# New pitches, latencies and planner settings for the static instruction order of a two-layer linear-attention and gated-MLP kernel

**The chip, the cores and the metric.** The kernel runs on one core of one Trainium2 chip. The metric is the device time of one execution in microseconds. The profiled span, from the first to the last instruction of the core, is about 1.7 us shorter (1109.5 us in the run that took 1111.19 us).

## The reference

Two identical layers act on 2048 tokens of width 576: a linear attention with 32 heads of 18, then a gated MLP of inner width 4608. Shortened:

```python
phi_q = concat(softmax(pq), softmax(-pq))      # pq = q @ w_phi per head, head width 18
phi_k = concat(softmax(pk), softmax(-pk))
kv  = einsum("bhsf,bhsd->bhfd", phi_k, v);  z = phi_k summed over s
o   = (phi_q @ kv) / (phi_q @ z + 1e-6)
...
x = x + attention(layernorm(x), wqkv, w_phi, wo)
h = (layernorm(x) @ w_gate) * (layernorm(x) @ w_up)
x = x + h @ w_down
# the four lines are applied twice, with the same weights
```

The MLP needs all of kv, and so all 16 token tiles of 128, before its first block can start. Hence a "K phase" stands ahead of the first MLP, and a long stream of matmuls after it. Layer 2's attention is interleaved with the MLP of layer 1.

## The kernel before

The kernel is not written as loops over engines. Each task (a K tile, a query tile, an MLP block) is a generator that yields instructions with what they read and write. At build time a list scheduler walks through all of them with a model of the time, always takes the instruction whose estimated start (less a bias by priority) is the earliest, and appends it to the order of its engine. The chip then runs these fixed orders, with semaphores between the engines. The model's numbers therefore never cost anything on the chip; they only choose an order.

```python
SEM_LAT = 64.0                 # result of any engine is seen by any other after 64 ns
def ready_time(self, deps, eng=None):
    for d in deps:
        f = self.fin.get(d, 0.0) + (PE_SELF if eng == "pe" and d[0] == "pe" else SEM_LAT)
        ...
# an "alt" request: the planner may pick the engine
e_ = max(self.free_at[eng], tr.ready_time(deps), th.t_ready)
f_ = e_ + sum(o.dur for o in ops) * self.alt_cost[eng]     # earliest end wins; the first listed wins a tie
```

The softmax of one K tile, where the changed subtraction sits (the numbers are planned durations in ns):

```python
def softmax_front(self, st_, pz, Wm, km, crit, ...):
    # projection on TensorE into two PSUM banks, two ScalarE copies to SBUF (psb), then:
    VectorE  max of the SBUF copy (line 1030), 2 x min from PSUM (line 1035)
    GpSimd   d1 = psb - max            (line 1040, 1150)
    ...
    if crit == 1 and s.sub2pool:       # False before
        yield ("alt", [("dve", ops), ("pool", [Op(1150, d2 = psb - min)])])   # line 1054
    else:
        yield ("ops", "dve", ops)      # ops = 2 x 370: d2 = PSUM - min, line 1049
def softmax_tail(self, sm, crit, pz=None):
    ScalarE  exp of d2, exp of d1      (lines 1109, 1111)
    VectorE  sums of both              (line 1117)
    if crit > 1: VectorE reciprocal (line 1121)   else: ScalarE ln, exp (line 1124)
    GpSimd (or, if crit > 1, GpSimd or VectorE) 2 scalings   (line 1128)
    # afterwards TensorE accumulates K-V products of the tile (line 1170)
```

In one MLP block TensorE fills PSUM banks with gate and up products (line 1428, row-split: two 64-row matmuls run side by side), ScalarE copies the gate (line 1474), and VectorE multiplies it with the up product (line 1476), which frees the banks. Query projections (line 990 on the whole array, line 1002 row-split) are either done in the K phase or left to fill the MLP stream.

## Time and profile before

| what | before |
|---|---|
| time, median of 3 runs | 1112.03 us (1111.32 to 1113.44) |
| first gate/up matmul (line 1428) | 116.65 us |
| from there to the last epilogue (line 1544) | 989.1 us |
| layer-1 gate/up blocks 2 to 5, counted from 0, first to last matmul | 41.89 us (block 3: 42.09) |
| query tiles projected before the first gate/up matmul | 11 |

The prediction below shows the page, the stage table, and the waits of before. The chain of waits, the sequence of work that ended last, restricted to the K phase, can be followed back from 117 us to 56.5 us. Columns: start in us, length in us, engine, tile, line and number of instructions.

```profile
61.41 3.53 PE ps L990 x15
64.96 0.40 ACT psbx L1027
65.88 2.30 POOL dd L1128 x2
68.22 0.77 PE ps L1170 x10
...
81.75 1.26 DVE ss L1117
83.02 0.66 DVE mxmnx L1030
83.67 0.73 DVE mxmnx L1035 x2
...
99.93 1.75 POOL dd L1128
101.72 0.77 PE ps L1170 x10
102.49 1.23 PE ps L990 x10
```

The reader is to see three stretches. From 61 to 81 us TensorE, GpSimd, ScalarE and VectorE take turns. From 81 to 100 us every piece is VectorE. From 100 to 116.65 us it is one GpSimd scaling, then nearly only TensorE. Added up over the pieces from 56.5 to 116.65 us, VectorE has about 24 us of this chain, TensorE 25, GpSimd 6 and ScalarE 4. So VectorE is busy for 92% of the K phase, but it carries about 40% of the visible part of what sets its end. (The first piece is long for another reason: from 61.1 to 64.5 us the trace records a granted TensorE clock of 0.5. Ten such matmuls take 1.23 us elsewhere in this chain, so fifteen would take about 1.85 us instead of 3.53. The section on the experiments comes back to this.)

### The profile page before, as it was taken

The numbers are of one execution on the slowest core, as the hardware profiler recorded it, in microseconds if no ns is written. First come the engines' busy times: TensorE is split into PE (matmuls) and PEld (weight loads), VectorE is DVE, ScalarE is ACT, GpSimd is POOL, SyncE is SP. The second block draws the span as 40 slices with busy tenths as digits, with TensorE's granted clock in tenths as the row PEclk, the third lists the DMA queues.
The fourth block names the chain that finished last, engine by engine and source line by source line (L and its number), as shares of the span: only waits on it lengthen the run. The fifth ranks groups of instructions, "written<-read, shape, count | busy, mean of one in ns | idle before, by whom it ended". The sixth has DMA issues, their size and how long they took to land.

```text
span 1109.5 us, 33782 instructions
## 1 busy us (share of the span) xinstructions
PE 1072.4 (97%) x15342; PEld 832.2 (75%) x15342; DVE 586.1 (53%) x1192; ACT 373.7 (34%) x855; POOL 311.4 (28%) x330
## 2 busy tenths in 40 slices
PE   6787999999999999999999899999999999999998
PEld 4565886868687786869687678696969696969685
DVE  8998744646375564636453675444435353524231
ACT  6776631414133242404232463131313130402120
POOL 4885512414152432413220252211212130300000
PEclk9999999999999999999999999999999999999999
DMA  7595227273552616371523313727172726262504
GB/s 169 121 279 194 38 44 195 48 205 47 149 100 78 162 29 194 48 204 27 159 69 96 98 24 47 215 36 216 36 215 35 205 47 188 63 182 48 180 26 140
DMA packets 185002, 129.07 MB, mean 116 GB/s; under 512 B 103322, under 2 KB 183706, under 8 KB 183706
## 3 DMA queue, kind: packets, MB, share of 16 engines
q1 hardware_dynamic: 184858, 126.91, 44.6%
q8 instruction: 120, 1.97, 0.7%
q14 instruction: 24, 0.20, 0.1%
HBM read 100.75 MB, written 2.36 MB: 93 GB/s over the span
## 4 chain that ended last, share of the span: by engine, by line
PE 87%; DVE 4%; DMA 1%; ACT 1%; POOL 1%; issue 0%
PE ps L1428 50%; PE ps L1501 22%; PE ps L1002 7%; PE ps L1503 3%; PE ps L990 2%; PE ps L1289 2%; PE ps L1170 1%; DVE ss L1117 1%; POOL dd L1128 1%; DVE x_sb L1364 1%; DMA oT<-dd 1%; DMA wdr<-in_B_w_down_dram 0%; DMA wdx<-in_B_w_down_dram 0%; DVE mxmn L1035 0%; DVE dd L1049 0%
## 5 line engine op out<-in xcount | busy, mean ns | idle before, releaser
L1428 PE MATMUL ps<-xT,Wu 64*128 64x256 bf16 x4608 | 581.8, 269 | 0.0
L1428 PE MATMUL ps<-xT,Wg 64*128 64x256 bf16 x4608 | 579.2, 269 | 0.8 <-ACT xT L972 0.8
L1428 PEld LDWEIGHTS ps<-xT,Wu 64*128 64x128 bf16 x4608 | 431.5, 94 | 22.0 <-DVE hT L1476 0.3
L1428 PEld LDWEIGHTS ps<-xT,Wg 64*128 64x128 bf16 x4608 | 427.4, 94 | 27.4 <-issue 3.3
L1474 ACT CAST hT<-ps 128x512 bf16<-128x512 f32 x288 | 168.4, 585 | 568.5 <-PE ps L1428 541.7
L1476 DVE TENSOR_TENSOR hT<-ps,hT 128x512 bf16<-128x512 f32 x288 | 198.3, 690 | 240.7 <-ACT hT L1474 238.9
L1501 PE MATMUL ps<-wdr,hT 128*128 128x512 bf16 x960 | 245.2, 380 | 1.0 <-DMA wdr<-in_B_w_down_dram 1.0
L1503 PE MATMUL ps<-wdr,hT 128*128 128x64 bf16 x960 | 185.0, 193 | 0.0
L1428 PE MATMUL ps<-xT,Wr 64*128 64x256 bf16 x1152 | 184.9, 269 | 0.0
L1501 PEld LDWEIGHTS ps<-wdr,hT 128*128 128x128 bf16 x960 | 93.9, 98 | 111.1 <-DMA wdr<-in_B_w_down_dram 1.8
L1128 POOL TENSOR_TENSOR dd<-dd,ss 128x576 bf16<-128x576 bf16 x119 | 137.1, 1174 | 123.0 <-ACT ss L1124 119.0
L1099 POOL TENSOR_TENSOR dd<-xT,mxq 128x576 bf16<-128x576 bf16 x56 | 63.5, 1163 | 329.4 <-DVE mxq L1095 329.4
L1544 DVE TENSOR_TENSOR x_sb<-ps,x_sb 128x64 bf16<-128x64 f32 x32 | 7.0, 220 | 228.6 <-PE ps L1503 228.6
L962 POOL TENSOR_SCALAR xln<-x_sb,nmean,rstd 128x576 bf16<-128x576 bf16 x100 | 61.1, 616 | 182.1 <-ACT rstd L951 103.7
L1503 PEld LDWEIGHTS ps<-wdr,hT 128*128 128x128 bf16 x960 | 94.1, 98 | 0.2
L1117 DVE TENSOR_REDUCE ss<-dd 128x64 f32<-128x1152 bf16 x61 | 81.9, 1344 | 15.1 <-ACT dd L1111 15.0
L1428 PEld LDWEIGHTS ps<-xT,Wr 64*128 64x128 bf16 x1152 | 78.1, 94 | 5.2
L1501 PE MATMUL ps<-wdx,hT 128*128 128x512 bf16 x192 | 54.3, 380 | 0.1
L1109 ACT ACTIVATE dd<-dd 128x576 bf16<-128x576 bf16 x61 | 41.7, 684 | 32.8 <-DVE dd L1049 22.7
L1040 POOL TENSOR_TENSOR dd<-psb,mxmn 128x576 bf16<-128x576 bf16 x26 | 30.3, 1166 | 64.8 <-DVE mxmn L1030 64.8
L934 DVE BATCH_NORM_STATS2 st<-x_sb 128x6 f32<-128x288 bf16 x120 | 45.9, 444 | 2.4 <-DMA x_sb<-in_A_x_dram 2.4
L1002 PE MATMUL ps<-Wo,oT 64*128 64x288 bf16 x504 | 44.0, 283 | 1.2 <-DMA oT<-dd 0.4
(123 smaller groups left out, 970.0 us busy)
## 6 DMA issues: line engine op xcount, KB each, us to landing
wdr<-in_B_w_down_dram SPq DMA_DIRECT2D x240, 288.0 KB, 3.7
wdx<-in_B_w_down_dram SPq DMA_DIRECT2D x48, 288.0 KB, 3.7
Wg<-in_B_w_gate_dram SPq DMA_DIRECT2D x4, 1152.0 KB, 17.0
Wu<-in_B_w_up_dram SPq DMA_DIRECT2D x4, 1152.0 KB, 19.5
x_sb<-in_A_x_dram SPq DMA_DIRECT2D x8, 288.0 KB, 3.4
out_dram<-x_sb SPq DMA_DIRECT2D x16, 144.0 KB, 2.7
Wraw<-in_A_wqkv_dram SPq DMA_DIRECT2D x8, 144.0 KB, 2.8
xT<-xln SPq DMA_TRANSPOSE x58, 2.6
```

Source lines behind the costliest of these rows:

```text
L934: ops.append(Op(d_dve(288), (lambda e, j=j, h=h, src=src: e.bn_stats(st[:, sl[j], 6 * h:6 * h + 6], src)), reads=rd, writes=[("st", sl[j], ...
L962: em = [(lambda e, j=j, a=a, b=b, c=c: e.tensor_scalar(xln[:, sl[j], a:b], x_sb[:, ss[j], c:c + b - a], s.nmean[:, sl[j]:sl[j] + 1], rstd[ ...
L1002: out.append(Op(61, (lambda e, h=h, k=k, st=(i == 0 and k == 0), sp=(i == 1 and k == 3): e.matmul(s.ps[:, banks[h], 0:N], L[r, k, :], Wm[r ...
L1099: yield ("ops", "pool", [Op(1150, (lambda e, d=d, mb=mb: e.tensor_tensor(d, p3, mb, ALU.subtract)), reads=[("xT", st_), ("mq", mq, br)], w ...
L1109: yield ("ops", "act", [Op(590, (lambda e: e.activation(de2, de2, ACTF.Exp, scale=-1.0)), reads=s.ddk(sm, 1), writes=s.ddk(sm, 1))])
L1117: Op(1320, (lambda e: e.tensor_reduce(ss[:, sm, :].rearrange("p (b g) -> p b g", b=2), e4, AX.X, ALU.add)), reads=s.ddk(sm, 0) + s.ddk(sm, ...
L1128: yield ("alt", [(eng, [Op(dur, (lambda e, ev=ev, rb=rb: e.tensor_tensor(ev, ev, rb, ALU.mult)), reads=s.ddk(sm, br) + [("ss", sm)], write ...
L1428: out.append(Op(54.3, (lambda e, bank=bank, cs=cs, lhsT=lhsT, rhs=rhs, st=st, sp=sp: e.matmul(ps[:, bank, cs].rearrange("p (a n) -> p a n" ...
L1474: yield ("ops", "act", [Op(540, (lambda e, gb=gb, p=p: e.copy(hT[:, p, :], ps[:, gb, :])), reads=[("gu", gb)], writes=[("hT", p)] + (s.raw ...
L1476: yield ("ops", "dve", [Op(625, (lambda e, ub=ub, p=p: e.tensor_tensor(hT[:, p, :], ps[:, ub, :], hT[:, p, :], ALU.mult)), reads=[("gu", u ...
L1501: ops = [Op(d_pe(512), (lambda e: e.matmul(s.ps[:, bank, 0:512], lhsT, s.wslot(slot)[:, fi, 0:512], start=(f == 0), stop=(f == NF - 1))), ...
L1503: Op(d_pe(64) + 3, (lambda e: e.matmul(s.ps[:, z, 64 * sl:64 * sl + 64], lhsT, s.wslot(slot)[:, fi, 512:576], start=(f == 0 and (sl == 0 o ...
```

## The change

Its intent: the planner should know, for every engine, how long an instruction occupies it (pitch) apart from how long its result takes to be seen (latency); and the second subtraction of a K tile may go to GpSimd. The planner's settings were chosen anew with it. Core of the diff (cuts marked):

```diff
-SEM_LAT = 64.0
+LAT = {"pe": 200.0, "act": 145.0, "dve": 120.0, "pool": 90.0, "sp": 64.0}
-            f = ... (PE_SELF if eng == "pe" and d[0] == "pe" else SEM_LAT)
+            f = ... (PE_SELF if eng == "pe" and d[0] == "pe" else LAT.get(d[0], 64.0))
 def d_act(n, psum=False, ptrs=0):
-    return n / 1.2 + (63.0 if psum else 92.0) + 93.0 * ptrs
+    return n / 1.2 + 50.0
 def d_actc(n):
-    return n / 1.2 + 155.0
+    return n / 1.2 + 50.0
@@ settings
-        self.qlead = 8;  self.alt = 1.2; self.lnlead = 14; self.pqp = (5, 5); self.pqg = 12
+        self.qlead = 7;  self.alt = 1.1; self.lnlead = 9;  self.pqp = (3, 3); self.pqg = 6
-        self.qcrit = False; self.fq = 3; self.fqs = 2; self.fqp = 7.5; self.sub2pool = False
+        self.qcrit = True;  self.fq = 5; self.fqs = 1; self.fqp = 6.5; self.sub2pool = True
@@ planned durations: query max/min 720 -> 665, both exponentials 590 -> 560, sums 1320 -> 1265,
@@ gate copy 540 -> 480, gate product 625 -> 600   (each is one number in the code)
```

"Model" below means the latencies and durations, "settings" the two lines under it.

More of the change, by code (lines that the diff above doesn't have):

```diff
@@ L67, in ready_time @@
         for d in deps:
-            f = self.fin.get(d, 0.0) + (PE_SELF if eng == "pe" and d[0] == "pe" else SEM_LAT)
+            f = self.fin.get(d, 0.0) + (PE_SELF if eng == "pe" and d[0] == "pe" else LAT.get(d[0], 64.0))
             if f > t:
@@ L556, in __init__ @@
         self.early = (2, 2)
-        self.qlead = 8
-        self.alt = 1.2
-        self.wage = 0.0
+        self.qlead = 7
+        self.alt = 1.1
+        self.wage = 0
         self.lnage = 4
-        self.lnlead = 14
+        self.lnlead = 9
         self.pol0 = 1
@@ L564, in __init__ @@
         self.urgent = 4
-        self.pqp = (5, 5)
-        self.pqg = 12
+        self.pqp = (3, 3)
+        self.pqg = 6
         self.NPQ = 2
@@ L570, in __init__ @@
         self.pqn = (16, 16)
-        self.qcrit = False
-        self.fq = 3
-        self.fqs = 2
-        self.fqp = 7.5
-        self.sub2pool = False
+        self.qcrit = True
+        self.fq = 5
+        self.fqs = 1
+        self.fqp = 6.5
+        self.sub2pool = True
         self.rboost = 500.0
@@ L1094, in stored_front @@
         for br, alu in ((0, ALU.max), (1, ALU.min)):
-            yield ("ops", "dve", [Op(720, (lambda e, br=br, alu=alu: e.tensor_reduce(s.mxq[:, mq, br, :], p3, AX.X, alu)), reads=[("xT", st_)], writes=[("mq", mq, br)])])
+            yield ("ops", "dve", [Op(665, (lambda e, br=br, alu=alu: e.tensor_reduce(s.mxq[:, mq, br, :], p3, AX.X, alu)), reads=[("xT", st_)], writes=[("mq", mq, br)])])
         for br in range(2):
@@ L1108, in softmax_tail @@
         de2 = dd[:, sm, 1, :]
-        yield ("ops", "act", [Op(590, (lambda e: e.activation(de2, de2, ACTF.Exp, scale=-1.0)),
+        yield ("ops", "act", [Op(560, (lambda e: e.activation(de2, de2, ACTF.Exp, scale=-1.0)),
                                  reads=s.ddk(sm, 1), writes=s.ddk(sm, 1))])
-        yield ("ops", "act", [Op(590, (lambda e: e.activation(de1, de1, ACTF.Exp)),
+        yield ("ops", "act", [Op(560, (lambda e: e.activation(de1, de1, ACTF.Exp)),
                                  reads=[("dd", sm, 0)], writes=[("dd", sm, 0)])])
@@ L1116, in softmax_tail @@
         yield ("ops", "dve", [
-            Op(1320, (lambda e: e.tensor_reduce(ss[:, sm, :].rearrange("p (b g) -> p b g", b=2), e4, AX.X, ALU.add)),
+            Op(1265, (lambda e: e.tensor_reduce(ss[:, sm, :].rearrange("p (b g) -> p b g", b=2), e4, AX.X, ALU.add)),
                reads=s.ddk(sm, 0) + s.ddk(sm, 1), writes=[("ss", sm)]),
@@ L1473, in t_bmain @@
                     p = 2 * q + i
-                    yield ("ops", "act", [Op(540, (lambda e, gb=gb, p=p: e.copy(hT[:, p, :], ps[:, gb, :])),
+                    yield ("ops", "act", [Op(480, (lambda e, gb=gb, p=p: e.copy(hT[:, p, :], ps[:, gb, :])),
                                              reads=[("gu", gb)], writes=[("hT", p)] + (s.raw_keys if (L, b) == (1, 0) else []), excl=[("pb", gb)])])
-                    yield ("ops", "dve", [Op(625, (lambda e, ub=ub, p=p: e.tensor_tensor(hT[:, p, :], ps[:, ub, :], hT[:, p, :], ALU.mult)),
+                    yield ("ops", "dve", [Op(600, (lambda e, ub=ub, p=p: e.tensor_tensor(hT[:, p, :], ps[:, ub, :], hT[:, p, :], ALU.mult)),
                                              reads=[("gu", ub), ("hT", p)], writes=[("hT", p)], excl=[("pb", ub)])])
```

## The prediction

> **What bounds the kernel now.** I read, in order: the page's engine totals, the 40 slices, a table of engine time by stage, the groups of instructions before and after 117 us, the timelines of VectorE and GpSimd between 60 and 105 us, and the waits of TensorE after 117 us.
>
> ```profile
> PE 1072.4 (97%) x15342; PEld 832.2 (75%) x15342; DVE 586.1 (53%) x1192; ACT 373.7 (34%) x855; POOL 311.4 (28%) x330
> ...
> PE   6787999999999999999999899999999999999998
> DVE  8998744646375564636453675444435353524231
> POOL 4885512414152432413220252211212130300000
> ```
>
> TensorE is busy 97% of the span; only the first four slices (28 us each) and the middle dip are lower. VectorE is at 80 to 90% only in those four slices. So there are two regimes, which the stage table separates:
>
> ```profile
> 5.00:30.00 25.00, 18.69 (x120) 12.73 (x120) 22.40 (x66) 18.11 (x53) 10.89 (x14) 1.00 0.74 174
> 30.00:60.00 30.00, 23.46 (x207) 16.84 (x207) 28.43 (x58) 21.61 (x59) 26.70 (x26) 0.94 0.51 112
> 60.00:102.00 42.00, 33.44 (x297) 24.18 (x298) 38.45 (x65) 30.76 (x82) 30.46 (x27) 0.96 0.80 266
> 102.00:117.00 15.00, 14.36 (x148) 10.67 (x147) 11.01 (x27) 9.56 (x24) 4.95 (x5) 1.00 0.35 110
> ```
>
> Columns: stretch, length, then busy time of PE, PEld, DVE, ACT and POOL, clock, DMA. From 5 to 102 us (the "K phase": norm, K and V projection, both softmax branches and the K-V product of 16 tiles) VectorE is busy 89.3 of 97 us. Its longest waits in that stretch are 1.5 us or less and together 9 us. From 102 to 117 us runs a dependent chain (last K-V product, block-diagonal state, numerators of tiles 0 and 1, output projection, norm, transpose); the first gate/up matmul starts at 116.65 us. After that TensorE waits only a little:
>
> ```profile
> PE ps L990 <- ACT xT L972: 1.6, 2, 0.8
> PE ps L1501 <- DMA wdr<-in_B_w_down_dram: 1.0, 2, 0.8
> PE ps L1428 <- ACT xT L972: 0.8, 1, 0.8
> PE ps L1344 <- ACT oT L1326: 0.6, 1, 0.6
> PE ps L990 <- ACT oT L1326: 0.5, 1, 0.5
> ```
>
> These five and three smaller ones are 5.7 us of waiting in 990 us. Everything after 117 us is a stream of matmuls, so only fewer matmuls in it, or an earlier start of it, shorten the program.
>
> The matmuls that could leave that stream are query projections of layer 1. Before 117 us:
>
> ```profile
> L990 PE MATMUL ps<-Wq,xT 128*128 128x288 bf16 x110 | 15.7, 287 | 2.8 <-DVE ddx L1049 2.0 <-ACT vxx L1155 0.5
> ```
>
> and after it:
>
> ```profile
> L990 PE MATMUL ps<-Wq,xT 128*128 128x288 bf16 x120 | 15.5, 286 | 0.0
> L1002 PE MATMUL ps<-Wq,xT 64*128 64x288 bf16 x162 | 14.4, 283 | 0.0
> ```
>
> A whole-array tile takes 10 such matmuls, a row-split one 18. So 11 tiles are projected before 117 us (tiles 0 and 1, and 9 stored ones), and 12 + 9 = 21 after it: 16 of layer 2 and 5 left over from layer 1.
>
> **What the Trainium skill says.** (1) "Perfetto Trace Analysis", Optimizing Scalar/DVE Operations: an instruction's profiled duration exceeds the time it holds the engine, because the write acknowledgement overlaps the next instruction. The trace agrees: the maximum (line 1030) has a mean of 745 ns, yet its successor starts 0.66 us after it; the pair of minima from PSUM (line 1035) lists 447 ns each and is followed after 0.73 to 0.74 us. This is the change's distinction of pitch and latency. (2) "TensorE: Matmul & The Clock Gate", Single matmul latency: (398 + N)/2.4 ns warm, thus 272 ns at N = 256. The trace has 269 ns, while a pair of row-split matmuls follows every 0.11 us. So a dependent waits some 0.2 us longer than the matmul's share of the array, and the old plan's 64 ns was too short. (3) "Trainium Kernel Development and Optimization", Key Constraints: GpSimd cannot access PSUM. Hence the subtraction moved to it must read the SBUF copy of the projection. (4) "SBUF — State Buffer", Who interferes with whom: a VectorE operation with two SBUF inputs contends with GpSimd's reads, one with at most one SBUF input outside the two-port modes does not. The trace fits: the PSUM subtraction (line 1049) stays at 442 to 448 ns in every group, whereas line 1128 on VectorE, two SBUF inputs, took 757 ns once and 1261 ns another time, with GpSimd working in that stretch.
>
> **The change part by part.** All instructions are laid out at build time by a list scheduler; the run executes fixed per-engine orders with semaphores. New durations and latencies thus cost nothing themselves. They can only reorder.
>
> 1. New estimates. Planned VectorE sums go 1320 to 1265 ns and query minima/maxima 720 to 665; exponentials 590 to 560; gate copies 540 to 480; gate products 625 to 600. The latency after VectorE becomes 120 ns instead of 64, so pitch plus latency for the sum is 1385 against 1384: the dependent's ready time is unchanged, only the engine is free 55 ns sooner. For the gate copy it is 625 against 604, close to the 585 ns plus semaphore that the trace shows. These are small corrections of a plan that already packs VectorE at 92%. I estimate 1 us saved.
>
> 2. Second subtraction to GpSimd (16 tiles in the K phase, 14 eligible, the last two take another path). On VectorE it is two instructions in 0.73 us (0.81 us in the merged timeline less the 80 ns overlap). On GpSimd it is one instruction of the same shape as line 1040, 1166 ns. If all 14 moved, VectorE would lose 10.2 us and GpSimd gain 16.3 us. But the scheduler chooses per tile the engine that finishes first, and the first subtraction of the same tile already sits on GpSimd. Right after the minimum VectorE ends its version about 0.8 us later, GpSimd about 1.65 us later (0.5 us to finish the first subtraction, then 1.15). GpSimd wins only where VectorE has been given another item first, typically a 1.27 us sum. GpSimd has 30.46 of 42 us and 26.70 of 30 us taken already. I choose 6 of 14: 6 x 0.73 = 4.4 us off VectorE, and 6 x 1.17 = 7 us onto GpSimd, which idles 11.5 us between 60 and 102 us. As VectorE sets the phase, the gate/up stream starts 4.4 us earlier.
>
> 3. Query projections may begin after tile 6 instead of 12 (group limit), at lower priority. TensorE has room: by spacing, a 288-wide matmul takes 0.123 us (1.23 us per ten), so K, V and Q projections before 117 us are 430 x 0.123 = 53 us, K-V products 16 x 0.62 = 10 us, the rest about 12 us: 75 of 117 us. So up to 5 leftover tiles can leave the saturated stream, each row-split one being 9 pairs x 0.122 = 1.1 us: 5.5 us at most. Limits are ScalarE (two 0.3 us copies a tile) and five free PSUM banks, the other three holding the K-V sums. I choose 4 tiles: 4.4 us.
>
> 4. Query weights are fused between tiles 5 and 9 rather than 3 and 11, norms of later tiles wait for tile b-9 rather than b-14, and the early query tiles get the critical path treatment: reciprocal on VectorE (543 ns) in place of two ScalarE activations (256 ns each), and a choice of engine for subtraction and scaling. This puts up to 2 x (0.46 + 0.75) = 2.4 us onto the engine that sets the phase; I charge 1 us.
>
> Sum: -1.0 - 4.4 - 4.4 + 1.0 = -8.8 us, so 1112 becomes 1103 us. No part touches the number of matmuls of lines 1428, 1501 and 1503.
>
> **The rivals.** (a) GpSimd becomes the bound. For: it takes 1.17 us for what VectorE does in 0.73, it was 89% busy from 30 to 60 us, and its scalings (line 1128) release the K-V product. Against: the choice is by finish time, and GpSimd idles 11.5 us afterwards. It would leave the phase unchanged; only the query projections help: about 1107. (b) The phase shrinks, but the stream cannot start because its weights arrive later. The eight big gate/up loads are issued between 63 and 68 us and the DMA stays near 390 to 490 GB/s until about 91 us; their start hangs on the last norm of layer 1. A later norm (lead 9) could push this back. Against: 25 us remain between 91 and 116.65. I expect no effect unless the last norm slips by more than 15 us. (c) All of it works: VectorE and GpSimd balance near 12 moved tiles (8.8 us), all five projections leave (5.5 us), the order gains 3 us: 1112 - 17.3 = 1095. (d) The new order delays a chain in the middle or at the layer boundary (617 to 651 us, already one dependent chain): plus 3 to 8 us, about 1112 to 1116.
>
> **Range and chances.** The centre is 1103. The upper end, 1111, stands for (a) with a small loss; the lower, 1094, for (c). A gain of 2% means below 1089.8, 22 us, which exceeds the sum of every term at its maximum (10.2 + 5.5 + 3 = 18.7 us): 3%. A loss of 2% means above 1134, which would need a phase grown by a fifth or a new hole in the matmul stream: 2%. Within 2%: 95%.
>
> **What would show it.** In the changed profile: the first matmul of line 1428 near 112 us (now 116.65); about 6 additional GpSimd subtractions before it, and about 12 fewer VectorE instructions of line 1049; 15 rather than 11 tiles of query projection before the stream, and about 17 rather than 21 after; the stream from its first gate/up matmul to the end shorter by about 4.4 us, its TensorE waits still near 6 us. If the start does not move although VectorE has less work, rival (a) holds; if GpSimd takes none, step 2 is void; if the waits after the start exceed 10 us, rival (d). My greatest uncertainty is the number of subtractions moved; the prediction fails if the phase is governed by a dependent chain rather than by VectorE's sum.

## The result

The changed kernel takes **1116.65 us** (median of 4 runs, 1114.62 to 1118.41) against 1111.7 us (4 runs, 1111.32 to 1113.44) for the kernel before. The ratio is 1.0041, with a 95% interval of 1.0017 to 1.0064: 0.4% slower, which is "same" by a threshold of 2%, but clear of the noise. Ratios here and below are the mean time of one kernel's fast runs over that of the other's of the same rounds, so not quite the ratio of the quoted medians. The predicted 1103 us and its range up to 1111 us were missed. The outputs are right.

The profiled runs have spans of 1109.5 and 1113.6 us. Of the 4.1 us between them, 1.7 us arise before the first gate/up matmul (116.65 to 118.33 us) and 2.4 us in the stream after it (989.1 to 991.5 us). So the start did not come 8 us earlier, and the stream did not shrink.

The page of the changed kernel, engine totals and slices:

```profile
PE 1065.9 (96%) x15280; PEld 820.7 (74%) x15342; DVE 589.2 (53%) x1193; ACT 372.5 (33%) x854; POOL 310.2 (28%) x328
...
PE   5687999999999999999999999999999999999998
...
DVE  7999744646475564635443575444534353524131
...
POOL 4875502415152432403321252121212030300000
```

The two regimes are where they were. VectorE's share in the first four slices has not gone down and GpSimd's has not gone up. (62 matmuls are missing from this trace: 15280 records against 15342 weight loads. Starts and stream lengths do not rest on them, and the query groups quoted here are whole.) The stage table, with the same columns as before (length; PE, PEld, DVE, ACT, POOL; clock; DMA share; GB/s):

```profile
5.00:30.00 25.00, 16.51 (x121) 11.94 (x122) 22.75 (x64) 17.71 (x51) 12.46 (x16) 0.93 0.78 182
30.00:60.00 30.00, 23.62 (x196) 17.07 (x196) 28.72 (x60) 21.34 (x60) 25.10 (x24) 0.89 0.50 121
60.00:102.00 42.00, 32.34 (x303) 24.10 (x303) 39.73 (x67) 30.61 (x82) 29.10 (x26) 1.00 0.80 283
```

VectorE is busy 91.2 of 97 us, before 89.3. The groups up to 118 us show how little of the change arrived:

```profile
L990 PE MATMUL ps<-Wq,xT 128*128 128x288 bf16 x100 | 13.7, 286 | 1.3 <-DVE dd L1049 1.3
...
L1054 POOL TENSOR_TENSOR ddx<-psb,mxmn 128x576 bf16<-128x576 bf16 x1 | 1.2, 1161 | 0.0
```

One subtraction moved to GpSimd, not six; line 1049 on VectorE fell from 36 to 34 instructions. Ten query tiles are projected ahead of the stream, not fifteen: one fewer than before. In exchange VectorE now has four reciprocals and four scalings in place of two and two, because the two early query tiles count as critical.

The end of the K phase on the changed kernel's chain of waits:

```profile
95.77 0.67 DVE dd L1049 x2
96.44 1.18 DVE dd L1128
97.62 2.52 DVE ss L1117 x2
100.14 0.87 DVE ss L1121 x2
101.01 1.46 DVE dd L1128
102.47 0.14 issue
102.61 0.76 PE ps L1170 x10
```

The last K-V product now waits for a VectorE scaling, one of two that together took 3.16 us on VectorE while GpSimd did two others in 2.80 us. In the kernel before, this place had one VectorE scaling of 0.76 us and the rest on GpSimd. From 56 to 118 us VectorE now has about 38 us of the chain, TensorE 16 and GpSimd none. The changed order has more of the chain on VectorE, not less.

Finally TensorE's waits from the first gate/up matmul on:

```profile
PE ps L1501 <- DMA wdr<-in_B_w_down_dram: 1.8, 2, 1.1
PE ps L1428 <- ACT xT L972: 1.6, 2, 0.8
PE ps L1170 <- POOL dd L1128: 1.2, 1, 1.2
PE ps L1428 <- DVE hT L1476: 0.8, 5, 0.2
...
PE ps L1503 <- ACT hT L1474: 0.7, 1, 0.7
```

All listed waits sum to 9.2 us, before to 5.6. New, among others, is the fourth line: five waits of up to 0.2 us for a gate product, which the list of before doesn't have.

### The profile page after: what moved, and what is told of

Its sections match the earlier page's. It is cut to its first block, busy times and chain, and to the rows that moved or that the text cites. A ratio compares the mean times of both kernels' runs of the same rounds, so it can differ in the third digit from the quotient of the medians.

```text
span 1113.6 us, 33723 instructions
## 1 busy us (share of the span) xinstructions
PE 1065.9 (96%) x15280; PEld 820.7 (74%) x15342; DVE 589.2 (53%) x1193; ACT 372.5 (33%) x854; POOL 310.2 (28%) x328
## 4 chain that ended last, share of the span: by engine, by line
PE 84%; DVE 6%; DMA 2%; ACT 1%; issue 1%; POOL 0%
PE ps L1428 49%; PE ps L1501 19%; PE ps L1002 7%; PE ps L1503 4%; PE ps L990 2%; PE ps L1289 2%; DMA wdx<-in_B_w_down_dram 1%; DVE ss L1117 1%; PE ps L1170 1%; DMA wdr<-in_B_w_down_dram 1%; DVE st L934 1%; DVE mxmn L1035 1%; DVE mxmn L1030 1%; DVE hT L1476 0%; DVE x_sb L1364 0%
## 5 line engine op out<-in xcount | busy, mean ns | idle before, releaser
L1501 PE MATMUL ps<-wdr,hT 128*128 128x512 bf16 x912 | 236.5, 380 | 1.8 <-DMA wdr<-in_B_w_down_dram 1.8
L1428 PE MATMUL ps<-xT,Wr 64*128 64x256 bf16 x1152 | 174.5, 269 | 0.0
L962 POOL TENSOR_SCALAR xln<-x_sb,nmean,rstd 128x576 bf16<-128x576 bf16 (+1 forms) x99 | 60.2, 612 | 210.9 <-ACT rstd L951 110.9
L1428 PEld LDWEIGHTS ps<-xT,Wr 64*128 64x128 bf16 x1152 | 71.8, 94 | 6.5
L1109 ACT ACTIVATE dd<-dd 128x576 bf16<-128x576 bf16 x61 | 41.7, 683 | 38.0 <-DVE dd L1049 26.5
L1501 PE MATMUL ps<-wdx,hT 128*128 128x512 bf16 x178 | 51.7, 380 | 0.3 <-DMA wdx<-in_B_w_down_dram 0.3
L1040 POOL TENSOR_TENSOR dd<-psb,mxmn 128x576 bf16<-128x576 bf16 x26 | 30.4, 1170 | 59.6 <-DVE mxmn L1030 59.6
L1111 ACT ACTIVATE dd<-dd 128x576 bf16<-128x576 bf16 x61 | 40.9, 671 | 0.0
```

The lines of the kernel that those rows point to most:

```text
L962: em = [(lambda e, j=j, a=a, b=b, c=c: e.tensor_scalar(xln[:, sl[j], a:b], x_sb[:, ss[j], c:c + b - a], s.nmean[:, sl[j]:sl[j] + 1], rstd[ ...
L1109: yield ("ops", "act", [Op(560, (lambda e: e.activation(de2, de2, ACTF.Exp, scale=-1.0)), reads=s.ddk(sm, 1), writes=s.ddk(sm, 1))])
L1428: out.append(Op(54.3, (lambda e, bank=bank, cs=cs, lhsT=lhsT, rhs=rhs, st=st, sp=sp: e.matmul(ps[:, bank, cs].rearrange("p (a n) -> p a n" ...
L1501: ops = [Op(d_pe(512), (lambda e: e.matmul(s.ps[:, bank, 0:512], lhsT, s.wslot(slot)[:, fi, 0:512], start=(f == 0), stop=(f == NF - 1))), ...
```

## The experiments

Each run has its own label. "Start" is the first matmul of line 1428 in the profiled run, "stream" the time from there to the last epilogue, "block" the length of layer-1 gate/up blocks 2 to 5, "tiles" the query tiles projected before the stream. Times are medians; each ratio is to the kernel before, on the same chip. Start, stream and block come from one profile per run. e11 has the same order as the changed kernel on every engine up to the stream, and its start differs from it by 0.53 us (117.80 against 118.33), so differences of half a microsecond in a start say nothing.

| run | time us | ratio (95%) | start | stream | block | tiles |
|---|---|---|---|---|---|---|
| before | 1111.7 | 1 | 116.65 | 989.1 | 41.89 | 11 |
| changed | 1116.65 | 1.0041 (1.0017 to 1.0064) | 118.33 | 991.5 | 42.22 | 10 |
| e1 model only | 1125.72 | 1.0114 (1.0095 to 1.0134) | 128.85 | 992.6 | 42.22 | 10 |
| e2 settings only | 1119.15 | 1.0054 (1.0036 to 1.0073) | 128.04 | 985.3 | 41.89 | 14 |
| e3 changed, no critical queries | 1121.92 | 1.0076 (1.0056 to 1.0097) | 126.45 | 990.4 | 42.22 | 11 |
| e8 changed, no moved subtraction | 1113.74 | 1.0024 (0.9995 to 1.0053) | 119.18 | 989.6 | 42.22 | 12 |
| e4 before, 7 subtractions forced | 1132.5 | 1.0181 (1.0161 to 1.02) | 140.23 | 986.4 | 41.89 | 13 |
| e7 as e4, scalings halved | 1121.64 | 1.0095 (1.0059 to 1.0131) | 130.23 | 984.4 | 41.89 | 13 |
| e5 before, sums halved | 1107.78 | 0.9971 (0.9942 to 0.9999) | 113.17 | 989.0 | 41.89 | 11 |
| e6 before, scalings halved | 1109.22 | 0.9984 (0.9941 to 1.0026) | 112.78 | 989.1 | 41.89 | 11 |
| e9 before, both halved | 1105.76 | 0.9934 (0.9895 to 0.9974) | 109.62 | 989.9 | 41.9 | 11 |
| e10 changed, VectorE scalings halved | 1115.7 | 1.0024 (0.998 to 1.0067) | 118.01 | 993.4 | 42.22 | 10 |
| e11 changed, old gate durations | 1115.01 | 1.0018 (0.9973 to 1.0062) | 117.80 | 990.6 | 42.16 | 10 |
| e12 changed, dearer VectorE scaling | 1114.35 | 1.0012 (0.9964 to 1.0059) | 117.92 | 989.6 | 42.22 | 12 |
| m3 changed, TensorE latency 64 | 1126.31 | 1.0133 (1.0113 to 1.0153) | 130.52 | 990.4 | 42.53 | 11 |
| m2 changed, all latencies 64 | 1128.9 | 1.0156 (1.0136 to 1.0177) | 128.98 | 994.1 | 42.59 | 12 |
| n1 before, new latencies only | 1118.44 | 1.0058 (1.0041 to 1.0075) | 122.01 | 990.2 | 41.89 | 10 |
| n2 before, new durations only | 1128.24 | 1.0142 (1.012 to 1.0163) | 125.34 | 999.1 | 42.59 | 10 |
| g1 settings searched | 1111.1 | 0.9997 (0.9984 to 1.0011) | 119.36 | 986.3 | 42.16 | 12 |
| g2 settings searched, no critical queries | 1111.93 | 1.0001 (0.9984 to 1.0017) | 116.74 | 987.4 | 42.16 | 11 |

The first theory was that model and settings only fit each other, and that the planned order as a whole moved the start. Its rival was that single parts add up: the moved subtraction, the critical queries, VectorE contended by GpSimd.

No run tested a second rival, TensorE's granted clock. In these traces it falls to 0.5 in the K phase for stretches of 3.4 us or a multiple of it. Up to the start these add up to 6.8 us in before, 10.2 in the changed kernel, 3.5 in e5, none in e6, 6.8 in e9, 10.2 in e7, 17 to 27 in e1, e2, e3, m2, m3, n1 and n2, and 41 in e4. So late starts mostly go with more time at half clock. Whether that time made them late, or both came from a TensorE that waited more, is not shown. It can't be the whole cause: e7 has as little of it as the changed kernel and starts 12 us later, while e10, in the changed kernel's order with shorter scalings, has 20.4 us of it and starts no later (118.01 us). But where a run differs much in this, its start is no clean price of the work that was taken out.

### Which part of the change moved the time: e1, e2, e3, e8

**e1** keeps the new latencies and durations and puts every setting of before back.

```diff
 # changed kernel
-        self.qlead = 7; ... self.pqg = 6; self.qcrit = True; ... self.sub2pool = True
+        self.qlead = 8; ... self.pqg = 12; self.qcrit = False; ... self.sub2pool = False
```

> The new durations and latencies alone, all planner settings as before. Theory 1 (VectorE's total work up to the last sum sets the first gate/up matmul, and the settings, above all the critical-path treatment of the early query tiles, added work there): the first matmul of line 1428 stays within 1.5 us of before's 116.65 us. Rival (the new latencies themselves made the first phase worse): it starts at 118 us or later. For the stream after that (992.5 us from first gate/up matmul to the last epilogue in before, 995 in the changed kernel): if the latencies make it longer it takes 994.5 us or more here, if the settings do it takes about 992.5. Time: 1110 to 1115 us.

Measured: 1125.72 us, start 128.85 us, 12.2 us later than before: the rival of the expectation held, by far more than it had asked for. The stream, 992.6 us, is 3.5 us longer than before's, of which the one query tile fewer ahead of it can account for about 1.1 us; so the new model lengthens it. (The 992.5 and 995 us of the expectation are counted to the end of the span, some 3.5 us more than here.)

**e2** is the opposite: old latencies and durations, new settings.

```diff
 # kernel before
-        self.qlead = 8; ... self.qcrit = False; ... self.sub2pool = False
+        self.qlead = 7; ... self.qcrit = True;  ... self.sub2pool = True
```

> The new settings with the old durations and latencies. Static order: 14 query tiles before the stream (before 11, changed 10), 2 subtractions on GpSimd, 4 reciprocals and 4 scalings on VectorE before the state is built (before 2 and 2). Theory 1: the start is later than before, 117.5 to 119 us, because of the added VectorE work; the stream is 3 x 1.1 us shorter than before for the three tiles more that left it, so the time is about that of before, 1110 to 1113 us. Rival (the model did the damage): start at 116 us or earlier and time 1105 to 1109.

Measured: 1119.15 us, start 128.04 us, 11.4 us later than before, though the stream is 3.9 us shorter, with 14 query tiles ahead of it. Neither theory of the expectation had a start so late. Here two subtractions went to GpSimd.

Alone, the halves cost 12.2 and 11.4 us of start; together they cost 1.7. So the two halves have no values of their own that could be added, which is how the prediction had added its parts. Together they largely cancel. This fits settings that were picked for their model; it would also fit starts that scatter with any change of the plan, of which each kernel shows a well-chosen one. The runs do not tell these two apart.

**e3** takes the critical treatment of the two early query tiles out of the changed kernel.

```diff
-        self.qcrit = True
+        self.qcrit = False
```

> The changed kernel with the critical-path treatment of the early query tiles off: 2 reciprocals and 3 scalings on VectorE before the state instead of 4 and 4. Theory 1: that takes 2 x 0.46 + 1.2 to 1.6 us off VectorE and the start moves from 118.3 to about 116 us; time about 1112 to 1114. Rival (a dependent chain, not VectorE's sum, governs the phase): the start stays at 118 us or more.

Measured: start 126.45 us, 8.1 us later, and 1121.92 us. That was a miss, and in sign: the prediction charged 1 us for this treatment, and taking it away costs 8 in this order.

**e8** forbids the subtraction on GpSimd in the changed kernel.

```diff
-        self.sub2pool = True
+        self.sub2pool = False
```

> The changed kernel with the choice of GpSimd for the second subtraction forbidden. Only 1 of 14 tiles used it, so by content the start would move by under 1 us from 118.33 and the time stay within 1 us of 1116.65. If the placing of a single instruction reshuffles what the greedy planner does afterwards, the static order says 12 instead of 10 query tiles before the stream, 14 instead of 10 norm instructions on VectorE; the start then moves by several us, probably later (120 to 125), and the time is 1115 to 1121.

Measured: start 0.85 us later, stream 1.9 us shorter, 1113.74 us; its interval reaches from before to the changed kernel, so no difference to either is shown. But the order differs by far more than the one instruction: with it, ten query tiles are projected before the stream; without it, twelve.

### Does VectorE's sum set the K phase: e4 to e7, e9

**e4** forces the second subtraction of every even K tile (7 of the 14) onto GpSimd, with everything else as before.

```diff
 # kernel before
-        self.sub2pool = False
+        self.sub2pool = True
-        if crit == 1 and s.sub2pool:
+        if crit == 1 and s.sub2pool and st_ % 2 == 0:
-            yield ("alt", [("dve", ops), ("pool", [Op(1150, ...)])])
+            yield ("alt", [("pool", [Op(1150, ...)])])
```

> The kernel before with the second subtraction of the 7 even tiles put on GpSimd without a choice. It takes 14 instructions of line 1049 (7 x 0.73 = 5.1 us) off VectorE. Theory 1 (VectorE's sum sets the phase): the start comes 3 to 5 us earlier, at 111.5 to 113.5 us, and 13 instead of 11 query tiles precede it, so the time falls by 4 to 7 us to 1105 to 1108. Rival (GpSimd or the dependent chain through it is the bound already): start at 116 us or later, time 1111 or more.

Measured: start 140.23 us, 23.6 us later; the first theory had expected it 3 to 5 us earlier. VectorE has 7 x 0.73 = 5.1 us less to do, and the phase grows by almost five times that. Its waits up to 140 us (columns: total us, times, longest us):

```profile
POOL dd L1128 <- ACT ss L1124: 21.9, 10, 5.0
...
PE ps L1170 <- POOL dd L1128: 13.6, 7, 4.1
DVE Wq L870 <- PE ps L864: 12.1, 4, 4.5
```

This reads as a circle: TensorE's fixed order holds at a K-V product (line 1170) until a late GpSimd scaling arrives; behind it stand the matmuls that fuse the query weights (line 864); VectorE's fixed order holds at their evictions (line 870), in front of the minima and sums that GpSimd needs next. Before, TensorE waited 4.8 us for the scalings up to 117 us, and VectorE never more than 1.5 us for anything between 5 and 102 us.

**e5** leaves the order of before and halves VectorE's sums in the layer-1 tiles (9 of 18 elements are added; the output stayed within the tolerance).

```diff
-  e.tensor_reduce(ss[...], e4, AX.X, ALU.add)
+  e.tensor_reduce(ss[...], e4[:, :, :, 0:DH // 2] if kph else e4, AX.X, ALU.add)   # kph: layer-1 K tile
```

> The order of the kernel before, instruction for instruction, but the 18 sums of line 1117 on the layer-1 tiles read only half of each head (576 instead of 1152 elements), so each holds VectorE about 0.6 us less: 16 x 0.6 = 9.6 us off VectorE before the state is built. The result is wrong on purpose. Theory 1 (VectorE's sum of work sets the first gate/up matmul): it moves from 116.65 to about 107 to 109 us. Theory 2 (a loop of waits through GpSimd's scaling and TensorE's fixed order sets it): it moves by under 3 us.

Measured: sixteen sums fall from about 1.34 to 0.74 us, which takes 16 x 0.6 = 9.6 us off VectorE. The start comes 3.5 us earlier: 0.36 us per us. That lies between the two theories (7.7 to 9.7 us, and under 3), but far from VectorE's sum setting the phase.

```profile
L1117 DVE TENSOR_REDUCE ss<-dd 128x64 f32<-128x576 bf16 x13 | 9.6, 739 | 4.1 <-ACT dd L1111 4.1
```

**e6** halves the GpSimd scalings instead (16 of 32 heads).

```diff
-  e.tensor_tensor(ev, ev, rb, ALU.mult)
+  e.tensor_tensor(ev[:, 0:16, :] if kph else ev, ..., rb[:, 0:16, :] if kph else rb, ALU.mult)
```

> The same order again, but the scalings of line 1128 on the layer-1 tiles cover half the elements: about 0.57 us less on each of some 30 GpSimd instructions, 17 us off GpSimd, almost nothing off VectorE. Result wrong on purpose. Theory 1: the start stays within 2 us of 116.65, since VectorE still has its whole work. Theory 2: it moves forward by 5 us or more, and TensorE's waits for GpSimd (5.1 us in before) vanish.

Measured: thirty scalings fall from 1.18 to 0.68 us, 15 us off GpSimd; the start comes 3.9 us earlier, 0.26 us per us, again between the two theories (within 2 us, and 5 or more). Both prices are probably too high: the stretch at half clock of before (61.1 to 64.5 us), which lengthened its chain by an estimated 1.7 us (3.53 less 1.85), is absent in e5 and e6.

**e9** makes both edits at once.

> The order of the kernel before with both the sums of line 1117 and the scalings of line 1128 halved on the layer-1 tiles. Halving the sums alone moved the start by 3.5 us for about 10 us less on VectorE, halving the scalings alone by 3.9 us for some 17 us less on GpSimd. If these two engines take turns as the limit in one loop of waits, both together give more than the sum: 9 us or more, a start at 107 us or earlier. If a third thing (ScalarE, TensorE's order, the transfers) holds the loop, the two together give 7.4 us or less, a start at 109 us or later.

Measured: start 7.0 us earlier, against 3.5 + 3.9 = 7.4 for the sum of the single ones. Had VectorE been the one bound, e6 should have given nothing. Had the two been rivals for the bound, both at once should have given clearly more than the sum. Within the half microsecond of a start they add. One reading is that each sits in its own stretch of one chain (in before, GpSimd's pieces lie between 65 and 76 us and at 100 us, VectorE's mostly between 81 and 100 us). But the chain also moves: in e6 every piece from 54.9 to 73.5 us is VectorE's, and in e5 GpSimd has 9.7 us of it instead of 6.3. So the paths through the two engines are nearly equally long, and relieving one leaves the other. In e9 the chain can be followed over some 80 us up to the start of the stream; TensorE has 49 us of it, VectorE 13, ScalarE 12, GpSimd 5. So 25 us less work on two engines bought 7 us.

**e7** is e4 with the halved scalings of e6.

> The order of the run with 7 forced subtractions (start at 140.2 us, TensorE waited 13.6 us for GpSimd's scalings and VectorE 12.1 us for TensorE's query weights), with the scalings halved as in the run before this one. Theory 2 (the late scalings caused the 23.6 us loss, through TensorE's fixed order and then VectorE's): the start falls by 12 us or more, to 128 us or less. If the loss came from the order of VectorE and ScalarE alone, the start stays above 134 us.

Measured: start 130.23 us, 10 us earlier than e4; a little short of the 128 us or less that the GpSimd theory had asked for. The time at half clock fell with it, from 41 to 10.2 us, in the same order. Two stretches of the stage table, first of e4, then of e7 (the clock is the third number from the end):

```profile
30.00:60.00 30.00, 22.32 (x161) 15.99 (x159) 24.05 (x48) 19.50 (x54) 22.95 (x22) 0.75 0.43 106
60.00:102.00 42.00, 29.33 (x240) 21.23 (x239) 27.96 (x50) 22.98 (x66) 30.71 (x29) 0.85 0.78 270
```

```profile
30.00:60.00 30.00, 22.10 (x179) 16.02 (x179) 27.05 (x57) 21.41 (x61) 20.37 (x26) 0.89 0.50 117
60.00:102.00 42.00, 30.55 (x277) 22.44 (x276) 31.58 (x54) 25.67 (x69) 22.07 (x26) 0.96 0.71 258
```

So shorter scalings bring 10 us here and 3.9 us in the order of before, which fits rival (a) of the prediction for e4; how much of the 10 us the scalings gave directly and how much the clock, the runs do not separate. The remaining 13.6 us over the kernel before stayed in this order; how they split was not settled.

### Is it contention between VectorE and GpSimd: e10, e12

**e10** halves only the scalings which the planner gave to VectorE in the changed kernel (the output is wrong).

```diff
-  e.tensor_tensor(ev, ev, rb, ALU.mult)
+  e.tensor_tensor(ev[:, 0:16, :], ev[:, 0:16, :], rb[:, 0:16, :], ALU.mult)   # VectorE version of a layer-1 K tile only
```

> The order of the changed kernel; only the few scalings that it gave to VectorE (4 before the state is built, planned at 675 ns, measured at 1.2 to 1.6 us because GpSimd reads at the same time) cover half the elements. Result wrong on purpose. If these contended scalings at the end of the phase are what the changed kernel lost there, the start moves from 118.3 to 116.5 us or earlier. If they are not on the path, it stays above 117.8.

Measured: the last two take 2.56 instead of 3.16 us, and the start moves from 118.33 to 118.01 us, no more than it differs between two runs of this order. **e12** tells the planner that a VectorE version costs 1250 ns instead of 675, which is nearer to what it took beside GpSimd.

```diff
-  for eng, dur in (("pool", 1150), ("dve", 675))
+  for eng, dur in (("pool", 1150), ("dve", 1250))
```

> The changed kernel, but the planner is told 1250 ns instead of 675 for a two-operand subtraction or scaling on VectorE. Static order: 3 such scalings on VectorE before the state instead of 4, 12 query tiles before the stream instead of 10. If the missing contention was the planner's remaining error, the time falls by 1 to 3 us against the changed kernel, to 1113 to 1115 us, with the start still near 118 us (two more query tiles lie before it).

Measured: start 117.92 us, stream 989.6 us, 1114.35 us, inside the expected 1113 to 1115; but the interval of its ratio, 0.9964 to 1.0059, is too wide to call it better than the changed kernel. The contention is real and visible, but it isn't what the 5 us are made of: in both runs the start moves by less than 0.5 us.

### Why the layer-1 gate/up blocks grew by 0.33 us: e11, m3, m2, n1, n2

In the changed kernel one stall of this kind stands in each of the blocks 2 to 5 (counted from 0), always 34.1 us after the block's first matmul. Here is the one at 405 us, first TensorE's timeline, then the chain of waits that ends at it (two views):

```profile
404.92 0.27 PE L1428 MATMUL ps<-xT,Wg 64*128 64x256 bf16 x1
405.25 0.28 PE L1428 MATMUL ps<-xT,Wu 64*128 64x256 bf16 x1
405.25 0.28 PE L1428 MATMUL ps<-xT,Wg 64*128 64x256 bf16 x1
```

```profile
403.11 0.75 DVE mxmn L1030
403.86 0.73 DVE mxmn L1035 x2
404.59 0.61 DVE hT L1476
405.20 0.05 issue
405.25 0.28 PE ps L1428
```

Pairs of row-split matmuls otherwise start every 0.11 us; here 0.33 us pass. The pair waits for a gate product, which frees PSUM banks, and in VectorE's order that product stands behind the maximum and minima of a layer-2 tile. The same block of before has no such gap inside. Which constant of the model made the planner believe the bank free in time?

**e11** puts the old durations of gate copy and product back (540 and 625).

> The changed kernel with the planned durations of gate copy and gate product back at 540 and 625 ns. The order before the stream is the same (10 query tiles, 1 subtraction on GpSimd), only the order within the gate/up blocks differs. If the shorter planned durations put matmuls where the bank is not yet free, the blocks 2 to 5 take 41.9 us again instead of 42.22 and the stream is about 1.5 us shorter than the changed kernel's 991.5 us. If the longer result latencies did it, the blocks stay at 42.2. The start stays at 118.3 within 1 us.

Measured: 42.16 us. That alone does not do it, and I then held the latencies responsible. **m3** and **m2** set TensorE's latency, then all four, back to 64 ns:

```diff
-LAT = {"pe": 200.0, "act": 145.0, "dve": 120.0, "pool": 90.0, "sp": 64.0}
+LAT = {"pe": 64.0, "act": 145.0, "dve": 120.0, "pool": 90.0, "sp": 64.0}     # m3
+LAT = {"pe": 64.0, "act": 64.0, "dve": 64.0, "pool": 64.0, "sp": 64.0}       # m2
```

> The changed kernel with the latency after TensorE alone set back from 200 to 64 ns; the other three new latencies stay. If TensorE's latency in the plan lengthens the layer-1 gate/up blocks, blocks 2 to 5 go back from 42.2 to 41.9 us; if the latencies after VectorE or ScalarE do it, they stay at 42.2. The start: the settings were presumably found with the 200 ns, so the theory that model and settings only work as a pair expects a start several microseconds later (122 to 132 us against 118.3) and 1118 to 1128 us in all; a theory that the 200 ns merely correct small errors of the plan expects the start within 2 us of 118.3.

> The changed kernel with all four latencies back to 64 ns, so only new durations and settings differ from before. If the latencies lengthen the layer-1 blocks, blocks 2 to 5 are 41.9 us; if not, 42.2. The start, by the theory that model and settings belong together, is later than 118.3 us, 122 to 132, and the time 1117 to 1128 us.

Measured: 42.53 and 42.59 us. The blocks became longer, not shorter, so the latency theory fell. Both starts moved beyond 128 us, as the theory that model and settings belong together had expected. **n1** and **n2** then split the model on the kernel before:

```diff
 # n1: kernel before
-SEM_LAT = 64.0
+LAT = {"pe": 200.0, ...}        # durations and settings as before
 # n2: kernel before
+the new d_act, d_actc and all new planned durations        # latencies and settings as before
```

> The kernel before with the new latencies only (old durations, old settings). If the new durations lengthen the gate/up blocks, blocks 2 to 5 stay at or below 41.9 us; if latencies do, 42.2. Start: the whole model gave 128.9 us with these settings; if the latencies alone upset the order, the start is 122 to 132 us and the time 1117 to 1127; if the durations do, 115 to 119 us and 1110 to 1114.

> The kernel before with the new durations only (old latency of 64 ns, old settings). If the new durations lengthen the gate/up blocks, blocks 2 to 5 are 42.4 to 42.6 us as in the run with all latencies back at 64; if not, 41.9. Start: 122 to 132 us if the durations upset the order; 115 to 119 if the latencies do. If each alone moves it by several microseconds, the order simply answers to any change of the model.

Measured: 41.89 us with new latencies alone, 42.59 with new durations alone. n2's blocks have two such stalls each, n1's none. So the shorter durations lengthen the blocks, and the longer latencies undo about half of it: 42.59 to 42.22. The two halves of the model are meant for each other, pitch plus latency; but their sum no longer kept the bank safe in this place. Which of the durations it is was not separated (the gate's two alone are not it). As to the start, each half alone delays it, by 5.4 and 8.7 us. That is the case of n2's last sentence: the order answers to any change of the model.

### Settings searched for the new model: g1 and g2

If the settings must fit the model, better-fitting ones might bring the start forward.

```diff
 # changed kernel, both: gate durations of before, VectorE alternatives at 1250
-        self.alt = 1.1; self.fq = 5; self.fqs = 1; self.fqp = 6.5
+        self.alt = 1.0; self.fq = 4; self.fqs = 2; self.fqp = 7.5
 # g2 also
-        self.pqp = (3, 3); self.qcrit = True
+        self.pqp = (5, 5); self.qcrit = False
```

> The changed kernel with settings searched for its own latencies: query weights fused between tiles 4 and 6, its priority 7.5, alternative factor 1.0, the planner's cost of VectorE's two-input alternatives 1250 instead of 675 ns, gate durations as before the change. Four subtractions on GpSimd, 12 query tiles before the stream. If the planned order is what moved the start, it comes near 113 to 116 us and the time to 1106 to 1111 us, faster than both kernels; if the work on VectorE and GpSimd were the cause of the late start, it stays at 118 us or later and 1113 us or more, because four moved subtractions load GpSimd more.

> As the run before, but early query tiles lose the critical treatment and their projection's lead goes back to 5: 11 query tiles before the stream. If the planned order is the cause: start 112 to 116 us and 1105 to 1111 us. If critical treatment of early queries is needed with the new model whatever the other settings (taking it from the changed kernel alone cost 8 us of start): start 124 us or later and 1116 us or more.

Measured: 1111.1 and 1111.93 us, ratios 0.9997 and 1.0001 of five runs each with intervals within 0.2%: the same as before, no better. Both starts missed the expectation of 112 to 116 us (119.36 and 116.74). g1's gain over the changed kernel lies in the stream, 986.3 against 991.5 us, with 12 tiles ahead of it instead of 10, and no wait for a weight transfer in TensorE's list. Four subtractions moved here, and the start was no earlier for it. g2 shows that critical queries are not needed as such: without them this order starts at 116.74 us, and e3's at 126.45. So the 5 us loss of the changed kernel can be undone by other settings together with three planned durations (both runs also change those of the gate copy, the gate product and VectorE's alternatives), but a kernel that beats before was not found.

## Why the prediction was wrong

**The step that failed** is the second: "As VectorE sets the phase, the gate/up stream starts 4.4 us earlier." It holds two claims. The count, "I choose 6 of 14", was 1: the planner compares planned ends, VectorE's version is listed first and planned at 2 x 370 x 1.1 = 814 ns, GpSimd's at 1150 ns behind the first subtraction, and only once was VectorE that much later. The greater fault is the other claim. A busy share of 92% was read as "sets the phase". If it did, the 9.6 us that e5 took off VectorE would have brought about 9.6 us; they brought 3.5. e5 and e6 give the price of work in the order of before: at most 0.36 us of start per us on VectorE and 0.26 per us on GpSimd. An estimate from these: a moved subtraction is worth -0.73 x 0.36 + 1.17 x 0.26 = +0.04 us, nothing that these runs could resolve, and no gain. And where the move was forced, it cost 23.6 us (e4), of which 10 went again when the scalings were halved (e7). The prediction's last sentence named this danger ("the prediction fails if the phase is governed by a dependent chain rather than by VectorE's sum"), but gave it no weight in the centre. (Two readings on the way were loose as well: VectorE's waits up to 102 us are "together" at most 7.7 us, its idle time in 97 us, not 9. And the 269 ns of a matmul are no independent check of the 272, since the profile models the ends of matmuls.)

**Step 1**, new estimates at -1.0 us: wrong in size and sign. It argued that pitch plus latency stayed nearly the same, so the order would too. With the settings of before, the model costs 12.2 us of start (e1), the latencies alone 5.4 (n1), the durations alone 8.7 (n2). A likely reason, argued from the planner's code and not tested: in a greedy order some tens of ns decide which of two instructions goes first, and everything after it follows. The durations also put a stall into each of the layer-1 blocks 2 to 5, which together are 1.1 us longer (block 3 of before was 42.09 us). The rest of the stream's 2.4 us is a sum of small gains and losses: the gap between blocks 6 and 7 grew by 1.4 us and two later gaps by 0.4 and 0.85; block 1 is 0.5 us longer and the first block of layer 2 1.1 us shorter, as a row-split query tile of 18 matmuls moved from the one to the other; and the very first block is 0.6 us shorter.

**Step 3**, 4 leftover query tiles for 4.4 us: the count went the other way, 11 to 10. The term itself was roughly sized: with 14 tiles ahead of it (e2) the stream is 3.9 us shorter, which is 1.3 us a tile. But it isn't free. The prediction gave TensorE "room" by a sum, 75 of 117 us, as it had judged VectorE by one. In the chain of before TensorE has nearly everything from 101.7 us to the start, and 5 of the 11 query tiles are projected just there, at 1.23 to 1.33 us each; a tile placed there leaves the stream, but not the chain. In every run that got 13 or 14 tiles ahead, the start was later by more than the stream won.

**Step 4**, early critical queries at +1.0 us: two more reciprocals and two more scalings did go to VectorE, and the last two scalings do take 3.16 us beside GpSimd. Yet removing the treatment costs 8 us in this order (e3), while g2 without it starts 2.6 us earlier than g1 with it (the lead of the early queries differs too, and one tile fewer lies ahead). No sign of its own can be read from this.

**The rivals.** (d), the new order delays a chain, gave 1112 to 1116 us, and is nearest to the 1116.65; but its own sign, over 10 us of waits after the start, was just missed at 9.2. (a) did not arise in the changed kernel, where GpSimd has less to do than before from 30 to 102 us (54.2 against 57.2 us); it arose when the move was forced. (b), gate/up weights too late for the start, did not arise: the eight loads were issued between 60.8 and 65.2 us, earlier than before, and the first gate/up matmul waited 0.8 us for ScalarE's copy of xT and not for a transfer. (c), all of it works, fell with steps 2 and 3. That the change lies within 2% held.

**What stays open**: what exactly sets each of the starts between 116 and 131 us. No part of the change has a fixed effect on it; that it belongs to the planned order as a whole is what the runs fit best, but no single wait was found that explains a start, and the part of the granted clock is untested.

## What to carry to other kernels

Before counting on an offload, read how much of the chain of waits the unloaded engine holds; shortening its work without touching the order, as e5 did, then gives the price per microsecond, and the receiving engine has such a price too. Compare the granted clock of the two runs before the price is believed. In a kernel ordered by a greedy planner, model and settings are one thing: more exact numbers with old settings may lose, so judge them only after the settings have been searched again, and against the scatter of neighbouring settings. And look for new small waits that repeat in every block: a third of a microsecond in each of four blocks was invisible in the busy shares and cost two thirds of what the later start did.

## What the Trainium skill lacked or had wrong

- "Perfetto Trace Analysis", Optimizing Scalar/DVE Operations, says that offloading may make sense if the engine is saturated, and that between VectorE and GpSimd it might not help. It gives no test for it. Here a VectorE that was busy for 92% of the phase returned at most 0.36 us per us taken off it (9.6 us off, 3.5 us won), GpSimd at most 0.26, and seven moved subtractions cost 23.6 us.
- The same section puts VectorE's overhead on PSUM at about 125 ns and says that the write acknowledgement, about as long again, overlaps with the next instruction. The overlap measured here is smaller: two minima from PSUM of 446 ns each take 0.81 us together, an overlap of 0.08 us. (They write to SBUF, for which the section gives about 60 ns; the maximum, which reads SBUF, also overlaps by 0.08 us: 742 ns, its successor 0.66 us after it.)
- "SBUF — State Buffer", Who interferes with whom: nothing wrong; it calls the shared port pair an exclusive lock and says that the order of issue decides who blocks, but has no durations for this pair of operations. In before, a VectorE scaling that began 0.05 us ahead of GpSimd's took 757 ns and GpSimd's 1.73 us instead of 1.16; one that began 0.52 us after GpSimd's took 1.26 us and ended 0.62 us after it. In the changed kernel two in a row took 3.16 us while GpSimd did two in 2.80 us.
- No page has it: how far a fixed order of instructions answers to the planner's numbers. The same work started its stream anywhere from 116.65 to 130.52 us when latencies, durations or settings alone were changed.
